# Heads 6 to 10 in a fused attention and SwiGLU kernel: cluster products one gap sooner, six transpositions each one place later, one copy moved to ScalarE

## The chip, the cores and the metric

The kernel runs on one core of one Trainium2 chip. The metric is the device time of that core in microseconds (us): the median of three runs before the change was 322.65 us. All times in the text are microseconds unless they are marked ns.

## What is computed

The reference has two stages. The first is attention over 4 batches of 8 heads, 768 positions and 64 elements a head, in which a query sees only the keys of its own cluster. The cluster of a query or key is the nearest of 16 centroids of its head:

```python
q_assign = np.argmax(np.einsum('bhsd,hcd->bhsc', q_n, c_n), axis=-1)
k_assign = np.argmax(np.einsum('bhsd,hcd->bhsc', k_n, c_n), axis=-1)
mask = q_assign[:, :, :, None] == k_assign[:, :, None, :]
scores = np.where(mask, scale * np.matmul(q, k.transpose(0, 1, 3, 2)), -1000000000.0)
```

A softmax and the product with v follow. The second stage takes the 3072 rows of 512 elements that the first gives, divides each by its root mean square, and puts it through a SwiGLU network: a gate and a value product (512 to 1536), `silu(gate) * val`, and an output product (1536 to 512).

## The kernel before, in words

**Units, heads, gaps.** The rows are cut into 8 units (`UNITS`): a batch and one half of its queries, 384 columns. A unit runs its 8 heads one after the other. `attention` (L706) walks over gaps, three a head: in each it calls `scores`, which puts two matmuls of 384 columns on TensorE (tile `s`, L349) and one exponential of 768 columns on ScalarE (`pT`, L353). In the middle gap of each head the `pv` of the head before it follows: 18 small matmuls (tile `acc`, L369) and, after every second head, a reciprocal and a multiplication on VectorE (`inv` L376, `x` L378). After that the gap runs whatever hook stands at it. The engines take these instructions in the order in which the code issues them: the kernel sets its order by hand (`tc.manual_schedule()`), and each engine works through its own queue.

**Unit 0 has hooks alone.** In units 1 to 7 the gaps are filled with the SwiGLU work of the unit before. In unit 0 there is none yet, and the dictionary `first` says what each of its 24 gaps does; a gap that it does not name runs `more`, one matmul that only keeps TensorE busy (tile `warm`, L133), and a gap with `None` runs nothing.

**What the hooks of unit 0 do.** `trans(g, h, part)` turns the queries (part 0) or keys (part 1) of head 4g+h, 384 columns, by three TensorE transpositions into a PSUM tile `tq` (L222), and copies that to SBUF (`qkT`), on ScalarE (L228) or, with `nc.vector` as last argument, on VectorE (L226). GpSimd (the queue called POOL) later casts `qkT` into `kext` and `qext`, the operands of `scores` (L241), and casts v into `vbf` (L244). `pair_clusters(p)` computes the cluster assignments of heads 2p and 2p+1: eight TensorE matmuls into a PSUM tile `sc` (L321), then on VectorE a transposition (L324), a maximum (L327) and a comparison into `pads` (L328). `head(n)` calls `under` twice, two VectorE transpositions (L333) that put head n's one-hot clusters under its keys and queries. The scores of a head can't start before both. `second_batch` (L649) issues on the SP queue a small transfer that reads `inv` (the one of heads 2 and 3), and behind it the loads of head 13.

**The list `late`** holds the eight calls of `trans` for heads 8 to 11, keys ahead of queries. The first six stand in gaps of unit 0; `late[6]` runs in the first gap of unit 1 (L712) with its copy on ScalarE, and `late[7]` in the second (L746), with its copy on VectorE.

**PSUM.** The tiles `tq`, `sc`, `warm`, `tx`, `gate`, `val` and `o` share the pool `ps_g` of three buffers, in turn, so each waits until the third tile before it has been read. The scores tile `s` has two buffers (`ps_s`), and `acc` has one (`ps_a`).

**The end of unit 0.** `pv(0, 7)`, the last of unit 0, is issued in the first gap of unit 1, behind `late[6]`. Then VectorE finishes `x`, its squares (L396) and their sum `ms` (L407); GpSimd takes a power for the inverse root (`yp`, L412); VectorE scales the rows (`xn`, L422); TensorE transposes them in `xtrans_all` (`tx`, L437); VectorE copies (L439); and the first gate and value products (L455) follow.

Of the kernel before, what the change touches and what calls it, by code (L numbers as in the profile page):

```python
# [22 lines left out]
def kernel(  # L23
# [12 lines left out]
    nc = tc.nc  # L36
# [8 lines left out]
    HG = 4  # L45
# [167 lines left out]
    def trans(g, h, part, on=None):  # L213
        if (g, h // 2) not in qkT:
            qkT[g, h // 2] = qk32.tile([P, 2, 2, UQ], F32, tag="qkT", name="qkT")
        qk = staged[g * HG + h]
        if g * HG + h >= BH:
            nc.vector.transpose(qkT[g, h // 2][:, h % 2, part], qk[:, part].rearrange("p t d -> p (t d)"))  # L218
            return
        ps = ps_g.tile([P, UQ], F32, tag="gen", name="tq")  # L220
        for i in range(HT):
            nc.tensor.transpose(ps[:, i * P:(i + 1) * P], qk[:, part, 2 * i:2 * i + 2].rearrange("p t d -> p (t d)"),  # L222
                                ident_f)
        to, by = qkT[g, h // 2][:, h % 2, part], 1.0 / ZS if part and g < BG else 1.0
        if on is nc.vector:
            nc.vector.tensor_scalar_mul(to, ps, by)  # L226
        else:
            nc.scalar.activation(to, ps, ACT.Copy, scale=by)  # L228
# [80 lines left out]
    def slot(n, m):  # L309

        return 32 * (2 * (n % 2) + m if n < 2 else 2 * m + n % 2)

    def pair_clusters(p, heads=(0, 1)):
        g, h = divmod(2 * p, HG)
        what = [(h + i, m) for i in heads for m in range(2)]
        at = [slot(2 * p + i, m) for i in heads for m in range(2)]
        r = slice(min(at), max(at) + 32)
        pool, tag = (ps_g, "gen") if p else (ps_s, "s") if 0 in heads else (ps_a, "acc")
        ps = pool.tile([P, 512], F32, tag=tag, name="sc")
        for a, (hh, m) in sorted(zip(at, what)):  # L320
            nc.tensor.matmul(ps[a:a + 32, :UQ], lhsT=cblk[:, g * HG + hh], rhs=qkT[g, hh // 2][:, hh % 2, m],  # L321
                             start=True, stop=True)
        sct = asg.tile([P, UQ], F32, tag="scT", name="scT", bufs=2)
        nc.vector.transpose(sct[r], ps[r, :UQ])  # L324
        cl = sct[r].rearrange("p (b e c) -> p b e c", e=2, c=NC)
        mx = ps[r, UQ:UQ + 2 * NB].rearrange("p (b e) -> p b e", e=2)
        nc.vector.tensor_reduce(mx, cl, axis=AX, op=ALU.max)  # L327
        nc.vector.tensor_tensor(pads[p][r, :, :NC].rearrange("p b c e -> p b e c"), cl,  # L328
                                mx.unsqueeze(3).broadcast_to([mx.shape[0], NB, 2, NC]), op=ALU.is_equal)

    def under(n, m):
        i = slot(n, m)
        nc.vector.transpose((kext if m else qext)[n // HG][D:D + 32, n % HG].bitcast(I32),  # L333
                            pads[n // 2][i:i + 32].rearrange("p b c e -> p (b c e)").bitcast(I32))
# [268 lines left out]
    def head(n):  # L603
        under(n, 1)
        under(n, 0)
# [38 lines left out]
    def more():  # L644
        busy(1, False)
# [3 lines left out]
    def second_batch():  # L649
        nc.sync.dma_start(out=hold, in_=invs[0].rearrange("p a t -> p (a t)"))  # L650
        load_qk(H + HG + 1)
# [29 lines left out]
    def gap8():  # L681
# [8 lines left out]
        for n in (6, 7):  # L690
# [2 lines left out]
        head(5)  # L693

    early = [lambda h=h, m=m: trans(1, h, m) for h in (2, 3) for m in (1, 0)]
    late = [lambda h=h, m=m: trans(2, h, m, nc.vector if (h, m) != (3, 1) else None) for h in range(HG) for m in (1, 0)]
    first = {0: lambda: trans(1, 1, 1), 1: gap1, 2: early[0], 3: early[1], 4: early[2], 5: gap5,
             7: lambda: head(4), 8: gap8, 10: None, 12: lambda: pair_clusters(3),
             13: lambda: (head(6), head(7)), 14: lambda: (more(), second_batch())}
    first.update({16: None, 19: None, 22: None, 23: None})  # L700
    first.update({i: f for i, f in zip((11, 15, 17, 18, 20, 21), late)})


    due = []
# [24 lines left out]
    for u in range(1, NU):  # L729
# [21 lines left out]
        else:  # L751
# [8 lines left out]
            n, m = {2: (8, 4), 3: (12, 4)}.get(u, (len(rows), len(clusters)))  # L760
# [45 lines left out]
```

## Time and profile before

| What | Value |
|---|---|
| median of three runs | 322.65 us (322.54 to 323.13) |
| the profiled execution, its own time | 322.53 us |
| its span in the profile | 320.8 us |
| mean granted TensorE clock | 0.999 |
| busy: TensorE / ScalarE / VectorE / GpSimd | 98% / 71% / 67% / 43% |

The profile was taken from one execution. The span runs from its first to its last instruction, and 322.53 - 320.8 = 1.73 us of that execution lie outside it. Views give a start, a duration, the engine, the line, the tiles and a count; a bracket at the end of a row gives idle time of the engine ahead of it, and what ended that. Several equal instructions in a row are shown as one row with a count, and their durations overlap a little[...]. In single records of the trace, exponentials of 768 columns that follow each other start 0.70 us apart, though each lasts some 0.81.

### The profile page before, as it was taken

To read this page: it belongs to the slowest core of one execution; us is meant where nothing else is said; L and a number is where in the kernel's file an instruction comes from. 1 tells how busy PE (TensorE), PEld (TensorE's weight loads), DVE (VectorE), ACT (ScalarE), POOL (GpSimd) and SP (SyncE) were. 2 spreads that over 40 slices of the span, in tenths; PEclk is the share of its full clock that TensorE was granted. 3 is DMA by queue.
4 is the path that set the end of the run, shared out by engine and by line. 5 is a ranking of instruction groups with operands and counts; after the bars stand their busy time and mean duration, and the time that the engine had idled before them with its cause. 6 is when DMAs were issued, how large, how long until landed. Compare 5 with 4: busy or idle time off the path is not lost.

```text
span 320.8 us, 7736 instructions
## 1 busy us (share of the span) xinstructions
PE 315.3 (98%) x2831; PEld 190.8 (59%) x2845; DVE 215.4 (67%) x493; ACT 228.9 (71%) x420; POOL 136.3 (43%) x279
## 2 busy tenths in 40 slices
PE   8999999999999999999999999999999999999996
PEld 5657656565656556565566655665566656655554
DVE  5999789885678857779487767876266535681430
ACT  5999877976768767776769776886778767853321
POOL 5999678899524594048827074440000000000000
PEclk9999999999999999999999999999999999999999
DMA  7999995997555674567456340000500040005002
GB/s 256 375 264 182 167 199 121 231 135 117 90 131 129 172 111 75 111 132 167 69 94 147 110 114 35 13 14 1 150 1 2 2 114 35 0 2 147 3 0 100
DMA packets 91639, 34.64 MB, mean 108 GB/s; under 512 B 75600, under 2 KB 88528, under 8 KB 91600
## 3 DMA queue, kind: packets, MB, share of 16 engines
q1 hardware_dynamic: 84544, 27.84, 37.3%
q0 software_dynamic: 6768, 5.90, 10.5%
q8 instruction: 22, 0.36, 0.4%
q10 hardware_dynamic: 288, 0.39, 0.4%
q14 instruction: 17, 0.14, 0.2%
HBM read 28.61 MB, written 6.29 MB: 109 GB/s over the span
## 4 chain that ended last, share of the span: by engine, by line
PE 96%; ACT 3%; issue 1%; POOL 0%; ACTq 0%; POOLq 0%
PE s L349 19%; PE gate L455 19%; PE val L455 19%; PE o L493 18%; PE acc L369 11%; PE sc L255 3%; PE tq L222 2%; ACT pT L353 1%; PE warm L133 1%; ACT qkT L228 1%; PE o L504 1%; PE sc L321 1%; PE tx L437 0%; ACT o_sb L509 0%; PE c_ps L193 0%
## 5 line engine op out<-in xcount | busy, mean ns | idle before, releaser
L353 ACT ACTIVATE pT<-s 128x768 bf16<-128x768 f32 x192 | 154.7, 814 | 37.6 <-PE s L349 36.0
L349 PE MATMUL s<-qext,kext 80*128 80x384 bf16 x384 | 94.5, 328 | 0.1
L455 PE MATMUL gate<-xnT,wg 128*128 128x384 bf16 x384 | 78.5, 325 | 0.0
L455 PE MATMUL val<-xnT,wv 128*128 128x384 bf16 x384 | 78.4, 325 | 0.0
L493 PE MATMUL o<-wo,gvT 128*128 128x512 bf16 x262 | 66.0, 378 | 0.8
L477 DVE SCALAR_TENSOR_TENSOR th<-th,gate 128x384 f32<-128x384 f32 x81 | 44.5, 550 | 32.8 <-ACT th L476 32.8
L349 PEld LDWEIGHTS <-kext 80*128 80x128 bf16 x384 | 36.3, 98 | 32.6 <-issue 5.7
L476 ACT ACTIVATE th<-gate 128x384 f32<-128x384 f32 x81 | 39.7, 491 | 16.8 <-PE gate L455 16.8
L481 DVE SCALAR_TENSOR_TENSOR gvT<-th,val 128x384 bf16<-128x384 f32 x81 | 44.5, 549 | 9.7 <-PE val L455 4.5
L455 PEld LDWEIGHTS <-wg 128*128 128x128 bf16 x384 | 36.3, 97 | 23.2
L455 PEld LDWEIGHTS <-wv 128*128 128x128 bf16 x384 | 35.7, 97 | 22.0
L369 PEld LDWEIGHTS <-pT 128*128 128x128 bf16 x1152 | 43.2, 97 | 9.1 <-DVE x L378 0.9
L369 PE MATMUL acc<-vbf,pT 128*128 128x65 bf16 x1152 | 45.5, 193 | 0.0
L241 POOL CAST qext<-qkT 64x384 bf16<-64x384 f32 x64 | 34.3, 543 | 16.9 <-DVE qkT L218 9.7
L493 PEld LDWEIGHTS <-gvT 128*128 128x128 bf16 x276 | 26.0, 97 | 26.1 <-issue 0.2
L298 POOL DMA_DIRECT2D qext<-oh x48 | 23.1, 488 | 36.6 <-DVE oh L287 36.6
L241 POOL CAST kext<-qkT 64x384 bf16<-64x384 f32 x62 | 33.4, 538 | 4.6 <-DVE qkT L226 2.4
L298 POOL DMA_DIRECT2D kext<-oh x48 | 23.1, 489 | 12.9 <-DVE oh L287 12.9
L496 ACT COPY o_sb<-o 128x512 f32<-128x512 f32 x23 | 13.5, 586 | 18.6 <-PE o L493 18.6
L376 DVE RECIPROCAL inv<-acc 128x6 f32<-128x6 f32 x32 | 6.0, 187 | 24.7 <-PE acc L369 24.4
L218 DVE STREAM_TRANSPOSE qkT<-qk 128x384 f32<-128x384 f32 x38 | 19.5, 551 | 0.0
L378 DVE TENSOR_TENSOR x<-acc,inv 128x384 f32<-128x384 f32 x32 | 17.8, 558 | 1.1
(80 smaller groups left out, 219.6 us busy)
## 6 DMA issues: line engine op xcount, KB each, us to landing
vs<-in_v_dram SPq DMA_DIRECT2D x32, 192.0 KB, 3.7
out_dram<-o_sb SPq DMA_DIRECT2D x23, 256.0 KB, 2.6
qk<-in_q_dram SPq DMA_DIRECT2D x76, 48.0 KB, 3.1
qk<-in_k_dram SPq DMA_DIRECT2D x76, 48.0 KB, 2.5
qk<-in_q_dram SPq DMA_DIRECT2D x13, 192.0 KB, 4.2
qk<-in_k_dram SPq DMA_DIRECT2D x11, 192.0 KB, 4.2
wg<-in_moe_w_gate_dram POOLq DMA_DIRECT2D x2, 768.0 KB, 7.2
wv<-in_moe_w_val_dram POOLq DMA_DIRECT2D x2, 768.0 KB, 11.2
```

Source lines behind the costliest of these rows:

```text
L218: nc.vector.transpose(qkT[g, h // 2][:, h % 2, part], qk[:, part].rearrange("p t d -> p (t d)"))
L241: on.tensor_copy(to, of)
L298: on.dma_start(out=ext[D:D + NC, h, e * UQ:(e + 1) * UQ], in_=put[g, m][32 * h + e * NC:32 * h + (e + 1) * NC])
L349: nc.tensor.matmul(ps[:, j, :w] if nt == HT else flat[:, j * w:(j + 1) * w], lhsT=cols(kext[g % 4][:KR, hh], g, kc // HT, kc % HT * P, (kc ...
L353: nc.scalar.activation(pT[u, h][:, n * i:n * i + n, :w], of, ACT.Exp, bias=-scale * ZS, scale=scale if g >= BG else scale * ZS)
L369: nc.tensor.matmul(acc[:, h % 2, t], lhsT=pT[u, h][:, kc, t * P:(t + 1) * P], rhs=vbf[g % 4][:, hh, kc % HT * 2 + kc // HT], start=i == 0 ...
L378: nc.vector.tensor_tensor(dst, acc[:, :, :nt, :D], inv[:, :, :nt].unsqueeze(3).broadcast_to([P, 2, nt, D]), op=ALU.mult)
L455: nc.tensor.matmul(ps, lhsT=(wv if val else wg)[:, c, f * P:(f + 1) * P], rhs=xnT[u][:, c], start=c == 0, stop=c == CC - 1)
L476: nc.scalar.activation(th, ps, ACT.Tanh, scale=0.5)
L477: nc.vector.scalar_tensor_tensor(th, th, 1.0, ps, op0=ALU.add, op1=ALU.mult)
L481: nc.vector.scalar_tensor_tensor(gvT[u][:, f, :n], gates[u], 0.5, ps, op0=ALU.mult, op1=ALU.mult)
L493: nc.tensor.matmul(outs[u], lhsT=gvT[u][:, f, t * P:(t + 1) * P], rhs=wo[:, f], start=f == 0, stop=f == FC - 1)
```

## The change

`pair_clusters(3)`, the cluster products of heads 6 and 7, moves from gap 12 to gap 11. Gap 12 is then empty. The six transpositions `late[0]` to `late[5]` stood in gaps 11, 15, 17, 18, 20 and 21, and now stand in gaps 15, 17, 18, 20, 21 and 23. The copy of the sixth (the queries of head 10, `(h, m) = (2, 0)`) is made by ScalarE instead of VectorE. No transposition, product or copy is added or removed: unit 0 has five empty gaps before and after, and one copy changes its engine.

```diff
-    late = [lambda h=h, m=m: trans(2, h, m, nc.vector if (h, m) != (3, 1) else None) for h in range(HG) for m in (1, 0)]
+    late = [lambda h=h, m=m: trans(2, h, m, nc.vector if (h, m) not in ((2, 0), (3, 1)) else None) for h in range(HG) for m in (1, 0)]
     first = {0: lambda: trans(1, 1, 1), 1: gap1, 2: early[0], 3: early[1], 4: early[2], 5: gap5,
-             7: lambda: head(4), 8: gap8, 10: None, 12: lambda: pair_clusters(3),
+             7: lambda: head(4), 8: gap8, 10: None, 11: lambda: pair_clusters(3),
              13: lambda: (head(6), head(7)), 14: lambda: (more(), second_batch())}
-    first.update({16: None, 19: None, 22: None, 23: None})
-    first.update({i: f for i, f in zip((11, 15, 17, 18, 20, 21), late)})
+    first.update({12: None, 16: None, 19: None, 22: None})
+    first.update({i: f for i, f in zip((15, 17, 18, 20, 21, 23), late)})
```

The hooks of unit 0 from gap 11 on, side by side (`pv` stands in gaps 13, 16, 19 and 22, ahead of the hook):

| gap | before | after |
|---|---|---|
| 11 | `late[0]` | `pair_clusters(3)` |
| 12 | `pair_clusters(3)` | - |
| 13 | `head(6)`, `head(7)` | the same |
| 14 | `more`, `second_batch` | the same |
| 15 | `late[1]` | `late[0]` |
| 17 | `late[2]` | `late[1]` |
| 18 | `late[3]` | `late[2]` |
| 20 | `late[4]` | `late[3]` |
| 21 | `late[5]` (VectorE) | `late[4]` |
| 23 | - | `late[5]` (ScalarE) |

## The prediction

> **What bounds the kernel now.** I read the busy shares first, then the waits of TensorE, then the time line of each engine from gap 11 of unit 0 (20.90 us) to the first gate product (37.84 us).
>
> ```profile
> PE 315.3 (98%) x2831; PEld 190.8 (59%) x2845; DVE 215.4 (67%) x493; ACT 228.9 (71%) x420; POOL 136.3 (43%) x279
> ```
>
> TensorE is the bound as a whole. Its list of waits is empty from 38 us to the end, and scores, gate, value and output products stand there at 0.16 to 0.22 us each, back to back. So an edit in unit 0 is worth what it moves the first gate product by, and no more. Ahead of it the waits name one:
>
> ```profile
> PE tx L437 <- ACT qkT L228: 0.4, 1, 0.4
> ```
>
> The name misleads: that ScalarE copy starts at 35.63 and ends with the wait by chance. The row that is really late is VectorE's first `xn` (35.58 to 36.07 in the single records), which can't start before GpSimd's power, which needs `ms`, and so back to `pv(0, 7)`. VectorE's rows there:
>
> ```profile
> 32.77 0.20 DVE L376 RECIPROCAL inv<-acc 128x6 f32<-128x6 f32 x1 [0.20 <-PE acc L369]
> 33.00 0.56 DVE L378 TENSOR_TENSOR x<-acc,inv 128x384 f32<-128x384 f32 x1
> ...
> 35.59 1.28 DVE L422 TENSOR_SCALAR xn<-x,yp 128x512 bf16<-128x512 f32 x3 [0.61 <-POOL yp L412]
> ```
>
> The reader is to see that VectorE had been idle for 0.20 when `pv(0, 7)` came in, so TensorE, not VectorE, sets this chain. From the end of `pv(0, 7)` to `tx` it has a fixed length: 36.13 - 32.73 = 3.40 us. The question becomes: when does `pv(0, 7)` end? In TensorE's rows it starts at 32.02:
>
> ```profile
> 30.81 1.04 PE L349 MATMUL s<-qext,kext 80*128 80x384 bf16 x4
> 31.69 0.49 PE L222 MATMUL tq<-ident_f,qk 128*128 128x128 f32 x3
> 32.02 0.71 PE L369 MATMUL acc<-vbf,pT 128*128 128x65 bf16 x18
> ```
>
> By start to start a pair of scores takes 0.34 us of TensorE, a transposition of a head's half 0.33, a `pv` 0.55, a warming matmul about 0.26, and cluster products 0.79, with 0.10 lost ahead of them. From 20.90 to 32.02 stand 14 scores, 7 `tq`, 4 `pv`, one `warm` and one `sc`: 4.76 + 2.31 + 2.20 + 0.26 + 0.89 = 10.42 of 11.12 us. Some **0.7 us of small waits** is all that any order of these could save ahead of `pv(0, 7)`. ScalarE shows where two of them reach the exponentials:
>
> ```profile
> 23.46 3.11 ACT L353 ACTIVATE pT<-s 128x768 bf16<-128x768 f32 x4 [0.36 <-PE s L349]
> 26.76 4.54 ACT L353 ACTIVATE pT<-s 128x768 bf16<-128x768 f32 x6 [0.19 <-PE s L349]
> ```
>
> The first lies behind the cluster products of gap 12, the second behind `pv(0, 4)`, which waited for `x` on VectorE (25.04 to 25.60) to give the `acc` buffer back. A third, 0.2 us, is in the chain that ended last: scores 24 start at 31.35, when exponential 22 frees its buffer, although TensorE was free at about 31.15.
>
> [...] `pv(0, 4)` at 25.66 holds scores 17 back to 26.22. So whatever stands ahead of `pv(0, 7)` in the queue counts. [...] For the copy that changes its engine, [...] The trace has 0.55 and 0.50, and I use its starts: the row after follows 0.47 later on VectorE and 0.37 later on ScalarE.
>
> **The change, part by part.**
>
> *Cluster products in gap 11.* They start behind scores 11, at 20.90 + 0.34 + 0.10 = 21.34, and end at 22.12. Scores 12 then start at 22.12 instead of 21.70; exponential 12 is 0.38 late (22.67 for 22.29), which costs nothing further, as exponential 13 is released sooner: gap 12 is empty, scores 13 start at 22.46 instead of 22.91, and exponential 13 at 22.67 + 0.70 = 23.37 instead of 23.46. On VectorE the transposition L324 starts at 22.60 instead of 23.08, since the copy of `late[0]` (0.47) is no longer ahead. So `x` ends at 25.12 instead of 25.60, and `head(6)` and `head(7)` end at 27.5 instead of 28.0.
>
> *`pv(0, 4)`.* With `late[0]` in gap 15 TensorE would reach it at 25.27. VectorE lets it go at 25.12. But it also needs v of head 4 from GpSimd:
>
> ```profile
> 24.90 0.51 POOL L244 CAST vbf<-vs 128x384 bf16<-128x384 f32 x1
> ```
>
> GpSimd works without a gap here and nothing in its queue moves, so `pv(0, 4)` starts at 25.46 for 25.66: a **gain of 0.20**. The next cast of v (27.22 to 27.73) holds `pv(0, 5)` to about 27.78 (before: 27.96).
>
> *The later places.* Onward TensorE alternates as before, 0.2 ahead: scores 20 at 28.33 (28.51), `late[3]` 28.67, scores 21 at 29.00, `late[4]` 29.34, scores 22 at 29.74 behind exponential 20, `pv(0, 6)` 30.08, scores 23 at 30.63 (30.81). Then gap 23, empty before, has the transposition `late[5]`: 30.97 to 31.30. It fills the 0.2 us that scores 24 waited for exponential 22, and 0.13 more. Scores 24 start at 31.30 (31.35), `late[6]` at 31.63, `pv(0, 7)` at 31.97 (32.02). Of the gain of 0.20, **0.05 is left**.
>
> *The copy on ScalarE.* It stands between exponentials 23 (31.17) and 24, at 31.87, and exponential 24 starts at 32.24 (32.06). Exponentials 24 to 28 and the copies between them are 0.18 later. `pv(0, 7)` needs none of them, only exponential 23. `pv(1, 0)` needs 24 to 26: it starts at 35.24 (35.05) and TensorE is free by 35.8, ahead of `tx` at 36.08. The first `tx` waits on ScalarE for the copy that ended at 35.04, then 35.23: no hold. Exponential 28 ends at 37.02, before scores 30 (about 37.4) need its buffer. Cost: nothing while that cover of 0.3 us lasts; without it, the whole 0.18.
>
> *VectorE* loses one copy (0.47) and ends its work ahead of the last reciprocal at about 32.0 instead of 32.5. It waits longer there, so this earns nothing. *Buffers:* a transposition waits until the third tile before it has been copied; on these times the tightest is `late[3]` (28.67) after the copy of `late[0]` (27.54 to 28.10), and behind it only scores 21 would wait. *Queues:* POOL and SP keep their order; its only tie is that `second_batch` waits for `inv`, now 0.48 earlier, and head 13's loads start that much sooner, behind nothing that unit 0 still needs.
>
> **Sum.** `tx` at 36.08 for 36.13, and everything after follows: -0.05 us, the profiled execution from 322.53 to 322.48. The median of the runs stands 0.12 above that execution, so I give **322.60 us**. What a measurement of this kernel can tell from no change is about 0.2%, 0.65 us.
>
> **Rivals.**
>
> 1. *Faster: the waits really go.* If [...] scores and exponentials fell into step, nearly all of the 0.7 us goes: 321.95. For it: three waits named above sit exactly where the change works. Against: it takes all of them, GpSimd's casts have their own fixed row, and gap 23 gets 0.33 of work that scores 24 must pass. Over 0.2% it has 6%.
>
> 2. *Slower: ScalarE becomes the bound at the seam of the units.* The copy in gap 23 sits in the only stretch where ScalarE has no idle time, 31.35 to 36.8 us. It costs 0.37, or 0.50 if nothing overlaps, and delays exponentials 24 to 28, `pv(1, 0)` and then `tx`. It decides from the point where ScalarE runs 0.37 late (the 36.13 - 35.76 that TensorE now stands idle ahead of `tx`). With `late[5]` also pushing scores 24 by its full 0.33, the loss is 0.33 to 0.83: 323.0 to 323.5, of which the upper end alone is over 0.2%. For it: copies and exponentials are packed there. Against: exponential 24 moves by 0.18 on my count, half the slack. 13%.
>
> 3. *The early cluster products cost more than they return.* Scores 12 late by 0.43 could stay late if exponential 13 follows 12 instead of leading: +0.38, 323.0. It is within 0.2% too. Against: TensorE has an empty gap 12 at once.
>
> **Chances and range.** The likeliest case, with both smaller misses around it, stays within 0.65 us: 0.81; faster 0.06, slower 0.13. The range takes in -0.45 (half of the waits and the spread of the runs) and +0.6 (rival 2 or 3 with that spread): 322.2 to 323.2.
>
> **What would show it.** Right: exponential 12 about 0.4 late and 13 no longer behind an idle 0.36; `pv(0, 4)` at about 25.46, just behind the cast of v; `pv(0, 7)` within 0.1 of 32.02; VectorE idle for about 0.7 ahead of the last reciprocal; no TensorE wait after 38 us. Wrong: `tx` off 36.1 by over 0.3, `tx` waiting for ScalarE, or a new TensorE wait in units 1 to 7.

## The result, and the profile after

The changed kernel takes **322.12 us** (17 runs, 321.51 to 322.68) where the kernel before takes 322.65 us (17 runs, 322.30 to 323.19). The ratio is 0.9980, 95% interval 0.9973 to 0.9988: **0.53 us faster**. The forecast was 322.60 with a range from 322.2 to 323.2, so the time lies below the range, and a gain of ten times the forecast one has to be found.

The profiled execution of the changed kernel has a span of 320.16 us (before: 320.75). First the part that the prediction was about. Its waits of TensorE between 10 and 40 us have one row, and from 38 us to the end none:

```profile
PE s L349 <- ACT pT L353: 0.2, 1, 0.2
```

That wait is scores 27, held by exponential 25, which the copy on ScalarE made 0.2 later. The time line of TensorE around the seam of the units, in the changed kernel (this execution reached its first exponential 0.24 us sooner, at 10.94 for 11.18, so add 0.24 to compare with times of before):

```profile
25.23 0.71 PE L369 MATMUL acc<-vbf,pT 128*128 128x65 bf16 x18
...
30.74 0.49 PE L222 MATMUL tq<-ident_f,qk 128*128 128x128 f32 x3
31.07 0.51 PE L349 MATMUL s<-qext,kext 80*128 80x384 bf16 x2
31.41 0.49 PE L222 MATMUL tq<-ident_f,qk 128*128 128x128 f32 x3
31.74 0.71 PE L369 MATMUL acc<-vbf,pT 128*128 128x65 bf16 x18
```

`pv(0, 4)` starts at 25.47 on the old scale (25.66 before, forecast 25.46), `late[5]` at 30.98, scores 24 at 31.31, `pv(0, 7)` at 31.98 (32.02 before, forecast 31.97). On VectorE and ScalarE the rows that answer to those shown of before:

```profile
32.48 0.20 DVE L376 RECIPROCAL inv<-acc 128x6 f32<-128x6 f32 x1 [0.33 <-PE acc L369]
32.71 0.56 DVE L378 TENSOR_TENSOR x<-acc,inv 128x384 f32<-128x384 f32 x1
```

```profile
22.48 9.27 ACT L353 ACTIVATE pT<-s 128x768 bf16<-128x768 f32 x12 [0.47 <-PE s L349]
31.64 0.48 ACT L228 ACTIVATE qkT<-tq 128x384 f32<-128x384 f32 x1
32.01 0.82 ACT L353 ACTIVATE pT<-s 128x768 bf16<-128x768 f32 x1
```

Exponential 12 is late, the eleven after it follow without an idle time that the view lists, and the copy stands between exponentials 23 and 24. `tx` starts 0.04 sooner than before, counted from the first exponential, and **of the 160 exponentials from 41 us to the end of attention 156 stand 0.04 sooner as well**. So in this pair of executions the gaps of unit 0 gave 0.04 us of the forecast 0.05, and the profiles show nothing more in the middle. Cut at three instructions, the two executions compare so:

| stretch | before | after |
|---|---|---|
| start of the span to the first exponential | 11.18 | 10.94 |
| first exponential to the first gate product | 26.66 | 26.61 |
| first gate product to the last output product (L504) | 279.54 | 279.54 |
| start of the last output product to the end of the span ("the tail") | 3.37 | 3.07 |

The start is the same code in both. The tail is too: the last output tile is copied and sent, and the last semaphore instructions of VectorE, ScalarE, GpSimd and SyncE (L801) start 3.27 to 3.32 us behind the last output product before and 2.96 to 3.04 after. The wait of SyncE (the queue SP) for the last transfer shows the difference. Its row gives the total wait, the number of waits and the longest, before and after:

```profile
SPq L801 <- DMA out_dram<-o_sb: 0.7, 1, 0.7
```

```profile
SPq L801 <- DMA out_dram<-o_sb: 0.4, 1, 0.4
```

The DMA queues in the 1.1 us in which the packets of that transfer run (318.2 to 319.3 us before, 317.9 to 319.0 after; q1 also carries the end of the transfer ahead of it) tell what lies beside it. A row gives packets, MB and share; the last row is the transfer, with its time to landing. Before:

```profile
q1 hardware_dynamic: 259, 0.12, 36.2%
q14 instruction: 1, 0.01, 2.8%
issues: line engine op xcount, KB each, median us to landing
out_dram<-o_sb SPq DMA_DIRECT2D x1, 64.0 KB, 1.8
```

After:

```profile
q1 hardware_dynamic: 269, 0.12, 37.3%
issues: line engine op xcount, KB each, median us to landing
out_dram<-o_sb SPq DMA_DIRECT2D x1, 64.0 KB, 1.5
```

The reader is to see one packet of 8 KB on queue 14, which the profile calls "instruction"; by that name it is taken here for a fetch of instructions. It starts 1.05 us after the last output product began, beside the last output's packets, and lasts 0.50. After the change that packet isn't there; one comes at 3.70, behind the last instruction of the span (3.07). Another packet of this queue, at 2.3 to 2.6, is in all twelve profiles.

Single records of the trace show what the transfer loses. Its landing is told by sixteen updates of its semaphore (the counter that SyncE waits for: its wait ends at 2.41 before and 2.11 after, 0.01 to 0.02 behind the last update). After the change they come 1.91 to 2.09 us behind the start of the last output product. Before, fifteen come at 1.93 to 2.12 and **the sixteenth at 2.40**: one update in sixteen is late, by the 0.3 us of the wait and of the tail. That the fetch holds it up was the author's guess, as the two come together; the packets' records name no engine.

That the place of such a fetch goes with the number of instructions on an engine was a guess at this point, for the runs to test; the change alters three of these numbers in the built program. VectorE has **699 instructions for 701**: the copy went to ScalarE, and one semaphore instruction is gone (the traces list 27 `TENSOR_SCALAR` for 28 and 209 `EVENT_SEMAPHORE` for 210). ScalarE has 567 for 566, and TensorE 5485 for 5486. From here the theories were: A, the gaps gave 0.04 and the rest lies at the ends; B, in most executions the gaps give the 0.5 us; C, which replaced A after the first four runs, the count of VectorE's instructions sets where that fetch lies.

### The profile page after: what moved, and what is told of

It reads as the page before. It is cut to its first block, busy times and chain, and to the rows that moved or that the text cites. A ratio compares the mean times of both kernels' runs of the same rounds, so it can differ in the third digit from the quotient of the medians.

```text
span 320.2 us, 7748 instructions
## 1 busy us (share of the span) xinstructions
PE 315.5 (99%) x2845; PEld 190.8 (60%) x2845; DVE 214.9 (67%) x492; ACT 229.1 (72%) x421; POOL 136.5 (43%) x279
## 4 chain that ended last, share of the span: by engine, by line
PE 95%; ACT 2%; POOL 1%; DVE 1%; issue 0%; POOLq 0%; ACTq 0%
PE gate L455 20%; PE val L455 20%; PE s L349 19%; PE o L493 19%; PE acc L369 11%; PE sc L255 3%; PE tq L222 2%; ACT pT L353 1%; PE warm L133 1%; PE o L504 1%; PE sc L321 1%; ACT qkT L228 1%; POOL kext L241 0%; PE tx L437 0%; POOL yp L412 0%
## 5 line engine op out<-in xcount | busy, mean ns | idle before, releaser
L493 PE MATMUL o<-wo,gvT 128*128 128x512 bf16 x276 | 67.7, 378 | 0.0
```

Of the source, the lines that this page charges most:

```text
L493: nc.tensor.matmul(outs[u], lhsT=gvT[u][:, f, t * P:(t + 1) * P], rhs=wo[:, f], start=f == 0, stop=f == FC - 1)
```

## The experiments

The kernel before had medians of 322.80, 322.81 and 322.76 us beside the three groups of runs (e1 to e4, e5 to e8, e9 and e10). All edits are against the kernel before unless the text says otherwise. The ratios are those of the measurement and not always the quotient of the two medians (e7: 322.27 over 322.81 is 0.9983). Each run was profiled in one execution, so its gaps and its tail stand for that execution alone.

**e1_before_again**: no edit.

> The kernel before, unchanged. Theory A (the gaps of unit 0 gave the change 0.04 us, as the two profiles show at the first tx; the other 0.5 us of its median lie at the start and the end of an execution, outside the edit): within 0.2 us of the other runs of the kernel before, and in its profile the first exponential and the last output landing stand anywhere within some 0.3 us of the ones seen, since they vary from one execution to the next. Theory B (in most executions the gaps cost the kernel before some 0.5 us that its one profile did not catch): the same time, but a profile in which TensorE waits between 20 and 36 us longer than in the first one.

322.62 us, ratio 1.000 (0.9990 to 1.0010). First exponential to first gate product 26.67, as in the first profile, so no hidden wait in the gaps. The tail is 3.78: the fetch comes at 1.33 here, and the sixteenth update of the last landing at 2.79. This execution also lost 0.43 between gate and last product, where a value product waited for VectorE once (0.2, at 91 us); ten of the twelve profiles show no loss in this stretch.

**e2_after_again**: the changed kernel, no edit.

> The changed kernel, unchanged. Theory A: if the 0.5 us were the start and the end of executions by chance, the ratio comes back to 1.000 (-0.05 us, +-0.2); if they go with this program they come again, and the profile shows them ahead of the first exponential or behind the last output product. Theory B: -0.5 us again, with the distance from the first exponential to the first gate product shorter than that of e1_before_again by some 0.5 us.

322.17 us, ratio 0.9983 (0.9974 to 0.9992). The gain comes again. The stretch of the gaps is 26.65, only 0.02 less than in e1, so B has nothing to stand on; the tail is 3.05, as in the first profile of this kernel. (In this one execution TensorE waited 0.65 for the DMA that brings `xnT`, at 118 us.)

**e3_products_alone**

```diff
-             ... 10: None, 12: lambda: pair_clusters(3),
+             ... 10: None, 11: lambda: pair_clusters(3),
-    first.update({i: f for i, f in zip((11, 15, 17, 18, 20, 21), late)})
+    first.update({i: f for i, f in zip((12, 15, 17, 18, 20, 21), late)})
```

> The cluster products of heads 6 and 7 in gap 11, and late[0] in gap 12 in exchange; the rest as before. My working: pv(0, 4) is let go by x no earlier than before, as the copy of late[0] now stands ahead of the reciprocal instead of ahead of the transposition of the products; exponential 12 is 0.4 later and 13 no sooner. Theory A: 0.0 us within 0.1 from the first exponential to the first gate product; the time of the kernel before. Theory B, if it is late[0] in gap 11 that waits for its load in most executions: about half of the gain or more, -0.3 us.

322.45 us, ratio 0.9990 (0.9982 to 0.9997). The gaps: 26.62 for 26.66, as worked out. Yet it is faster, and its tail is 3.30. Theory A had no number for that.

**e4_copy_on_vector**: the changed kernel, the copy of `late[5]` back on VectorE.

```diff
-    ... nc.vector if (h, m) not in ((2, 0), (3, 1)) else None) ...
+    ... nc.vector if (h, m) != (3, 1) else None) ...
```

> The changed kernel with the copy of late[5] back on VectorE. VectorE had 0.34 us idle ahead of the last reciprocal in the changed kernel, and the copy takes 0.47 there: pv(0, 7) is unmoved, the reciprocal some 0.1 later, exponentials 24 to 28 0.19 sooner. Theory A: from the first exponential to the first gate product +0.1 us against the changed kernel, and the time of the changed kernel within 0.2. Theory B, if ScalarE's copy is what pays: the gain is lost, the time of the kernel before.

322.42 us, ratio 0.9987 (0.9979 to 0.9995). The gaps are at 26.66, the tail at 3.28. Theory A had said within 0.2 us of the changed kernel; it is 0.25 slower than e2, so A missed here as it did in e3. Both e3 and e4 have 700 instructions on VectorE. Their fetch starts at 3.6 us behind the start of the last output product, and all sixteen updates of the last landing are there by 2.09. But in both VectorE's last `DRAIN`, one of the closing instructions of the program, starts 0.46 to 0.49 after the semaphore instruction ahead of it (0.11 in the changed kernel), and the program ends 0.21 to 0.23 later. This suggested theory C, which the next runs put to the test by the count alone.

**e5_change_two_more**: the changed kernel with two spare instructions on VectorE in unit 4.

```diff
+            if u == 4:
+                for x in range(2):
+                    nc.vector.memset(const.tile([P, 1], F32, name=f"spare{x}"), 0.0)
```

> The changed kernel with two more instructions on VectorE (memsets of one column, spare tiles, issued in unit 4 where VectorE has idle time), so that it has 701, as the kernel before (the changed one has 699). Theory C (the time follows VectorE's instruction count: with 701 a block of 8 KB of instructions is fetched 1.0 to 1.6 us after the last output product, beside the last output's transfer, which then lands 0.3 to 0.7 later; with 699 the fetch comes after it): -0.05 us against the kernel before, so 322.5 to 322.8, the tail behind the last output product 3.4 to 3.8 us for 3.06, and a fetch in it between 1.0 and 1.6. Theory B (the gaps are worth the 0.5 us): the time of the changed kernel, 322.15, and its tail of 3.06.

322.59 us, ratio 0.9995 (0.9987 to 1.0003): the gain is gone, with every gap of the change in place (26.65). The fetch is back at 1.05 us, the sixteenth update of the landing comes at 2.58, and the tail is 3.56. ScalarE and TensorE have the counts of the changed kernel (567 and 5485), so theirs do not set the tail. The wait for the last transfer, and the queues from 318.4 to 319.5 us:

```profile
SPq L804 <- DMA out_dram<-o_sb: 0.9, 1, 0.9
```

```profile
q1 hardware_dynamic: 275, 0.13, 40.1%
q14 instruction: 1, 0.01, 3.1%
out_dram<-o_sb SPq DMA_DIRECT2D x1, 64.0 KB, 2.0
```

**e6_before_one_more**: the edit of e5 with `range(1)`, on the kernel before.

> The kernel before with one such instruction more on VectorE: 702. Theory C: [...] the fetch lies some 5 us or more ahead of the last output's transfer: the tail falls from 3.4 or more to 3.06 us, and the time by 0.3 to 0.6, to 322.2 to 322.4, with all gaps as before. Theory B: 322.65 to 322.8, no change.

322.39 us, ratio 0.9986 (0.9979 to 0.9993): **one instruction more makes the kernel before faster by 0.42 us**, with its gaps unchanged (26.68). The tail is 3.07. The fetch lies where theory C put it. The trace has it alone in the window from 311 to 312.5 us, 6.3 us ahead of the last output product, while VectorE is idle (6.54 us, up to its last copy at 317.33):

```profile
q14 instruction: 1, 0.01, 2.1%
```

**e7_before_four_more**: the same with `range(4)`.

> The kernel before with four such instructions more: 705. Theory C: as with one more, the fetch lies ahead of the last transfers, the tail is 3.06, and the time 322.2 to 322.4. Theory B: 322.65 to 322.8, no change.

322.27 us, ratio 0.9986 (0.9978 to 0.9994); tail 3.07, the fetch 6.5 us ahead of the last output product. The gaps, which are those of before, take 26.77 here for 26.66: so much a single execution can differ by. By the tail e6 and e7 should come to the time of the changed kernel, and the gaps give that 0.04 more; they stand 0.1 to 0.2 above its 322.17 (e2). The small remainder is not accounted for, and no larger than what the intervals leave open.

**e8_shift_alone**

```diff
-    first.update({16: None, 19: None, 22: None, 23: None})
-    first.update({i: f for i, f in zip((11, 15, 17, 18, 20, 21), late)})
+    first.update({11: None, 16: None, 19: None, 22: None})
+    first.update({i: f for i, f in zip((15, 17, 18, 20, 21, 23), late)})
```

> Only the six transpositions in their later places, late[5] copied by VectorE, and the cluster products left in gap 12 (gap 11 empty): 700 instructions on VectorE. From the first exponential to the first gate product I expect 26.66 us, as before, within 0.1: scores 12 come sooner and 13 behind the products as before, x of heads 2 and 3 is 0.4 sooner, and gap 23 has a transposition. Theory C: the tail is 3.3 as in the two kernels with 700, and the time 322.35 to 322.5. Theory B: about 322.65, or a gain that shows between the first exponential and the first gate product.

322.52 us, ratio 0.9993 (0.9985 to 1.0001). The gaps take 26.77, which can't be told from before, as e7 has 26.77 with unchanged gaps; the tail is 3.29, as in the other kernels with 700. The interval of the time doesn't settle it, and the median is 0.02 above what C foresaw (322.35 to 322.5); the tail is what C foresaw, and B's gain in the gaps isn't there.

**e9_two_on_gpsimd**: the control. The changed kernel with the two memsets of e5 as `nc.gpsimd.memset`, at `u == 7` instead of `u == 4`.

> The control of e5_change_two_more: the changed kernel with the same two spare memsets on GpSimd, ahead of unit 7, where GpSimd has nothing left to do; VectorE keeps its 699 instructions. Theory C [...]: the time of the changed kernel, 322.1 to 322.25 within the runs' spread, the tail 3.06 us, no fetch between 1.0 and 1.6 us behind the last output product. Theory D (any two instructions, or any new program, shift the end): a tail of 3.3 to 3.8 us and 322.4 or more.

322.18 us, ratio 0.9981 (0.9971 to 0.9990): as the changed kernel. Tail 3.06, no fetch between 1.0 and 1.6. So the time goes with VectorE's count, and not with something being added; theory D, by which any two added instructions would do it, falls.

**e10_copy_alone**: the kernel before with the copy of `late[5]` on ScalarE, in gap 21 (the first line of the change alone).

> The kernel before with only the copy of late[5] moved to ScalarE, in its old place, gap 21. My working for the gaps: exponential 22 comes 0.37 later behind the copy, scores 24 wait for it, and pv(0, 7) and the first gate product are 0.3 to 0.4 later: 27.0 us from the first exponential to the first gate product for 26.66. Theory C: VectorE has 700 instructions, so the tail is 3.3 us, 0.1 to 0.5 less than with 701. Together 322.7 to 323.0. Theory B would have no gain at the end to set against the 0.37: 323.0 to 323.2.

322.77 us, ratio 1.0002 (0.9991 to 1.0012). ScalarE's and TensorE's time lines show a loss of rival 2's kind, a copy on ScalarE that holds the exponentials up:

```profile
30.50 0.48 ACT L228 ACTIVATE qkT<-tq 128x384 f32<-128x384 f32 x1
30.87 2.28 ACT L353 ACTIVATE pT<-s 128x768 bf16<-128x768 f32 x3
```

```profile
31.74 0.50 PE L349 MATMUL s<-qext,kext 80*128 80x384 bf16 x2 [0.40 <-ACT pT L353]
```

Scores 24 wait 0.40 for exponential 22, and the gaps take 27.04, 0.38 more than before. The tail is 3.28, for a mean of 3.57 with 701. A loss of 0.38 in the gaps and a gain of some 0.3 at the end nearly cancel: a time that says "no change" holds two changes.

All profiles by VectorE's count:

| instructions on VectorE | kernels | last update of the landing, us | tail, us |
|---|---|---|---|
| 699 | changed (two executions), e9 | 2.09, 2.08, 2.08 | 3.07, 3.05, 3.06 |
| 700 | e3, e4, e8, e10 | 2.09, 2.08, 2.08, 2.08 | 3.30, 3.28, 3.29, 3.28 |
| 701 | before (two executions), e5 | 2.40, 2.79, 2.58 | 3.37, 3.78, 3.56 |
| 702, 705 | e6, e7 | 2.08, 2.09 | 3.07, 3.07 |

Both columns count from the start of the last output product. From the last update to the end of the span it is 0.98 to 0.99 us by the unrounded times in every kernel but those with 700, where it is 1.20 to 1.21. So with 701 the late update accounts for the whole difference; with 700 the landing is on time, and the loss of 0.2 lies behind it.

No kernel here beats the changed one clearly: its tail is as short as the shortest seen, and of the gaps' small waits it took some 0.04.

## Why the prediction was wrong

**The step that failed** is in its first part: "an edit in unit 0 is worth what it moves the first gate product by, and no more". That reasoning put the end of the program at nothing, because its order was unchanged. The instruction counts of the engines weren't. The sum "`tx` at 36.08 for 36.13, and everything after follows" was right up to the last output product and wrong behind it. The mean tail with 701 instructions is (3.37 + 3.78 + 3.56) / 3 = 3.57, with 699 it is 3.06: 0.51 us, beside 0.04 from the gaps. Together 0.55, where 0.53 and (e2, against 322.80) 0.63 were measured. The prediction also took 0.65 us as the least that can be told from no change; with 17 runs of each kernel 0.53 could be told.

**The parts by themselves.** The gaps were right nearly row by row: on the scale of before, exponential 12 started at 22.72 (forecast 22.67), 13 at 23.43 (23.37), `pv(0, 4)` at 25.47 (25.46), scores 23 at 30.63 (30.63), `pv(0, 7)` at 31.98 (31.97), `tx` at 36.09 (36.08). GpSimd's cast of v ended last ahead of `pv(0, 4)`, but only just: scores 16 started at 25.05 and take 0.34, so TensorE came to `pv(0, 4)` at about 25.39 instead of 25.27, and the cast ended at 25.42. ScalarE's copy didn't reach `tx` from gap 23, as forecast; from gap 21 it did (e10). It did hold scores 27 for 0.2, a new TensorE wait in unit 1, which the prediction had named as a sign of being wrong; here it cost nothing. The 0.04 itself is not firmly measured: the second pair of profiles (e1, e2) gives 0.02, and the gaps of before took up to 0.1 more in one execution (e7). VectorE's idle time ahead of the last reciprocal was 0.33, not 0.7, since its last square took 0.91 instead of 0.55 in this execution; nothing waits for it.

**The rivals.** None looked at the end of the kernel. "Faster: the waits really go" is not what happened: the seven-tenths of small waits are still there but for some 0.04. A loss like that of rival 2 exists, but at another place and by another path: with the copy in gap 21, exponential 22 is late, and scores 24 wait for it ahead of `pv(0, 7)`. Rival 3, the early products, costs nothing (e3: 26.62). The place of the cause that theory C names was in sight: the page lists the queues with the word "instruction", and the end of the kernel waits for one transfer of 64 KB that has no cover (0.7 us, the row of SPq L801). Asking of every engine whether its number of instructions changes would have pointed there; the size of 0.5 us could not be read from the one profile of before.

**The fetches in the middle.** The page of before lists two queues as "instruction": queue 8 with packets of 16 KB (0.36 MB in 22), and queue 14, on which the fetch in question lies, with packets of 8192 bytes (0.14 MB in 17). From the first gate product to the last output product stand 20 of the first and 13 of the second, before and after alike, and TensorE's list of waits is empty from 38 us on in both. This stretch takes 279.54 to 279.60 us in ten of twelve executions. At the end a fetch does go with a loss: with 701 instructions the tail is 0.3 to 0.7 us longer than with 699.

**What stays open.** That the fetch that moves belongs to VectorE is argued from counts alone (e5 and e9 against the changed kernel, e6 against before; e5 and e6 change no other engine's number); the profile names no engine for it. What makes its place go with the count is not shown. Why one update in sixteen is late by as much as 0.3, 0.5 or 0.7 us was not found; the fetch itself lasts 0.31 to 0.54. Why VectorE's last `DRAIN` starts some 0.4 us later with a count of 700 was not tried.

## What to carry to other kernels

Where an edit moves a tuned kernel by a few tenths of a microsecond, cut the execution at fixed instructions and compare the stretches before believing that the edit's own stretch made the difference. An edit that adds or removes instructions on an engine can act outside its own stretch: here, with one or two instructions more or fewer on VectorE, a fetch of instructions stood at another place, and in the three executions that had it beside the last output's transfer the tail was 0.3 to 0.7 us longer. To separate the two, add spare instructions to that engine and, as a control, to another.

## What the runs showed that was not expected

- One spare memset on VectorE takes 0.42 us off the kernel before (e6), and two take most of the changed kernel's gain away (e5: 322.59 for 322.17).
- The same last transfer of 64 KB lands in 1.5 us with no instruction fetch beside it and in 1.8 to 2.2 with one of 8 KB beside it (before 1.8, e5 2.0, e1 2.2); of the sixteen updates that tell of its landing, just one is late.
- The start varies by more than the change: the first exponential stands 10.84 to 11.54 us behind the start of the span in twelve profiled executions, with the same code ahead of it. In the first profile of before the five transposing matmuls from 5.0 us on last 0.42 each (the last 0.32), in that of the changed kernel 0.27 to 0.30.
